# Weight and token preparation moved into the first two attention steps of an attention/convolution branch kernel

## The chip, the cores and the metric

The kernel runs on one core of one Trainium2 chip. The metric is the device time of one execution in microseconds; lower is better. A core has five engines that each work through their own queue in order: TensorE (PE, with its weight loads shown apart as PEld), VectorE (DVE), ScalarE (ACT), GpSimd (POOL) and SyncE (SP), and DMA engines that they issue transfers to. PE and ACT, DVE or POOL meet through semaphores; a waiting instruction holds up everything behind it on its own queue.

## The reference

For two sequences of 4000 tokens with 144 channels, the kernel computes a block and all of its gradients (for x and eight weight tensors). Cut to what matters:

```
xa = layernorm(x)
q, k, v = split(xa @ w_qkv)
p = softmax(q @ k.T * 144**-0.5)
glob = (p @ v) @ w_att_out
u, g = split(gelu(xa @ w_mlp_in))
loc = (u * conv5(layernorm(g), dw_csgu)) @ w_mlp_out
m = concat(glob, loc)
m = m + conv5(m, dw_merge)
out = x + m @ w_merge
```

`conv5` is a depthwise convolution over five tokens. The outputs are `out` and the vector-Jacobian product of this with `grad_out`.

## The kernel before

**Tiling.** Tokens lie as 125 partitions by 32 blocks (`PB` = 125, `NB` = 32). Channels are 128 plus a remainder of 16 (`DR`). The 128 main rows of the transposed normalized tokens are `xaT_m`, those of `grad_out` are `goT`. `R` is one 128-row tile that holds both remainders: the 16 of the tokens, and five shifted copies (80 rows) of those of `grad_out`, so that one matmul takes a remainder and a five-tap sum together.

**Stages.** For each sequence: the prologue (layernorm, transposes, weight products), `phase_att`, then a merge phase (`Merge`). Weights are folded first in `prep_weights`: `M1` is the product of the query and key weights (kept as `Q0`, `RW` and `M1T`), `Wvo` that of value and output weights, `VUT`, `VU` and `VUs` are merge weights times the five taps, `dgm`, `dgf` and `dgs` diagonal matrices for the convolution, `WiT` a transposed weight.

**The prologue of sequence 0**, in this program order: issue the loads of x (SP), build the identity and cleared tiles (POOL), issue the loads of `grad_out` (SP); for each of four groups of eight blocks the statistics (`ln_st`, L318, and `ln_mv`, L324 to L331, which takes a power on POOL, L330) and the normalization (`ln`, L336 on DVE and L338 on POOL); then all of `prep_weights`; then for each group the transposes of tokens (`xat`, L343 to L348) and of `grad_out` (`gs`, L313; `gm`, L306), evicted by ACT and DVE. Two PSUM pools of six buffers serve it (`ps_prep`, `pps`). They are closed before `ps_w` (three buffers) and `ps_yz` are opened.

**`phase_att`** runs 33 steps `t` of eight slots `s`. In step `t`, slots 0 to 3 compute the scores of block `t` (`S_pair`, L683, L684), which DVE turns into a running negative maximum (L688, L690) and ACT into exponentials in `Pbuf` (L691). `rescale` (L696 to L702) aligns the four chunks and issues the DMA transpose `PT` (L703) on SP; the pads of `Pbuf` and `Sbuf` are cleared by POOL with seven DMAs and two memsets (L633, L634). Slots 2 and 3 compute `Y` of block `t-1` from `PT` (L711), slots 4 to 7 its `dP_pair` (L733, L734; DVE L737 to `Sbuf`), followed by the transpose `ST` (L857). Slots 6 and 7 compute `Z` of block `t-2` (L753), and all but slots 2 and 3 accumulate X (L792, DVE L796, L798). `jit_mm` in slot 1 and `jit_tr` in slot 4 prepare block `t+1`: a projection into `qb` (L657) and its four transposes into `qt` (L667). `PT` is a single buffer: the transpose of block `t` waits until Y of block `t-1` has read it.

**Local units.** `local_units` returns a list of small pieces for the convolution branch and its gradient (`z_unit`, L412; `e_tanh`, L420; `dug_unit`, L444; and others). `local()` spreads them evenly over the slots of steps 0 to 30. The first units are PE-light rounds for blocks 30, 31, 0 and 1.

**What sets the order.** Each engine's queue is fixed when the kernel is built, by a scheduler that works through the program by priority. SP and ACT DMAs share eight completion semaphores in turn, so that a ninth DMA waits for the first of them to land. At the end of sequence 1, `F.weights` reads the spilled taps `sWr` again.

Of the kernel before, what the change touches and what calls it, by code (L numbers as in the profile page):

```python
# [7 lines left out]
BF = mybir.dt.bfloat16  # L8
# [100 lines left out]
def prep_weights(k, W):  # L109
    nc, tc = k.nc, k.tc  # L110
    wp, tp_, ps = k.wpool, k.wtmp, k.ps_prep
    ident = W.ident

    def load_k(ap, r0, C, name, eng, pool=None):
        return load_k_(k, pool or wp, ap, r0, C, name, eng)

    dwt = tp_.tile([5, 3 * D], BF, name="dwt")
    nc.scalar.dma_start(dwt[:, 0:2 * D], k.dw_merge)
    nc.scalar.dma_start(dwt[:, 2 * D:3 * D], k.dw_csgu)
    Wqkv = load_k(k.w_qkv, 0, 3 * D, "Wqkv", nc.scalar, tp_)  # L120
    Wo = load_k(k.w_att_out, 0, D, "Wo", nc.scalar, tp_)
    Wm = [load_k(k.w_merge, h * D, D, "Wm%d" % h, nc.scalar, tp_) for h in range(2)]
    Wl = load_k(k.w_mlp_out, 0, D, "Wl", nc.scalar, tp_)
    Wi = load_k(k.w_mlp_in, 0, 2 * D, "Wi", nc.scalar)
    W.Wi = Wi

    def transp(src, c0, name, pool=None):
        t = (pool or wp).tile([128, 2, D], BF, name=name)
        nc.gpsimd.memset(t[:, 1, :], 0.0)
        pt = ps.tile([128, 2, D], BF, tag="tp")  # L130
        for cc, (a, w) in enumerate(((0, 128), (128, DR))):
            nc.tensor.transpose(pt[0:w, cc, 0:128], src[:, 0, c0 + a:c0 + a + w], ident[:])
            nc.tensor.transpose(pt[0:w, cc, 128:D], src[0:DR, 1, c0 + a:c0 + a + w], ident[0:DR, 0:DR])
        nc.scalar.copy(t[:, 0, :], pt[:, 0, :])
        nc.scalar.copy(t[0:DR, 1, :], pt[0:DR, 1, :])
        return t

    W.cols = cols = wp.tile([128, 6, 5], F32, name="cols")
    nc.vector.memset(cols[:], 0.0)
    pc = ps.tile([128, 6, 8], BF, tag="tp")  # L140
    for s, (a, w) in enumerate(((0, 128), (128, DR), (144, 128), (272, DR), (288, 128), (416, DR))):
        nc.tensor.transpose(pc[0:w, s, 0:5], dwt[:, a:a + w], ident[0:5, 0:5])
    for s in range(6):
        w = DR if s % 2 else 128
        nc.vector.tensor_copy(cols[0:w, s, :], pc[0:w, s, 0:5])
    nc.vector.tensor_scalar(cols[:, 0:4, 2:3], cols[:, 0:4, 2:3], 1.0, None, op0=ALU.add)

    WqT = transp(Wqkv, 0, "WqT", tp_)
    WkT = transp(Wqkv, D, "WkT", tp_)
    WvT = transp(Wqkv, 2 * D, "WvT", tp_)  # L150
    WlT = transp(Wl, 0, "WlT", tp_)
    c = float(D) ** -0.5

    def fused(lhs_k, rhs_k, scale, name, pool=None):
        t = (pool or wp).tile([128, 2, D], BF, name=name)
        nc.gpsimd.memset(t[:, 1, :], 0.0)
        for mt, mw in ((0, 128), (1, DR)):
            pt = ps.tile([128, D], F32, tag="tp")
            for kt in range(2):
                nc.tensor.matmul(pt[0:mw, :], lhs_k[:, kt, mt * 128: mt * 128 + mw], rhs_k[:, kt, 0:D], start=(kt == 0), stop=(kt == 1))  # L160
            nc.scalar.activation(t[0:mw, mt, :], pt[0:mw, :], ACT.Copy, scale=scale)
        return t
    M1 = fused(WqT, WkT, c, "M1", tp_)
    W.M1T = fused(WkT, WqT, c, "M1T")
    W.Wvo_d = spill(k, fused(WvT, Wo, 1.0, "Wvo", tp_), "Wvo_d")
    WvoT = fused(Wo, WvT, 1.0, "WvoT", tp_)
    WT = [WvoT, WlT]

    sWm = []
    sWr = []  # L170
    for h in range(2):
        t = tp_.tile([128, 2, 5, D], BF, name="sWm%d" % h)
        for ch in range(2):
            for kk in range(5):
                if h == 0:
                    nc.vector.tensor_scalar(t[:, ch, kk, :], Wm[h][:, ch, :], cols[:, 2 * h + ch, kk:kk + 1], None, op0=ALU.mult)
                else:
                    nc.gpsimd.tensor_scalar(t[:, ch, kk, :], Wm[h][:, ch, :], cols[:, 2 * h + ch, kk:kk + 1], 1.0, op0=ALU.mult, op1=ALU.mult)
        sWm.append(t)
        r = tp_.tile([128, 2, 112], BF, name="sWr%d" % h)  # L180
        nc.gpsimd.memset(r[:, :, 0:32], 0.0)
        for kk in range(5):
            nc.gpsimd.tensor_copy(r[:, :, 32 + (4 - kk) * DR:32 + (5 - kk) * DR], t[:, :, kk, 128:D])
        sWr.append(r)
    W.sWm_d = [spill(k, sWm[h], "sWm_d%d" % h) for h in range(2)]
    W.sWr_d = [spill(k, sWr[h], "sWr_d%d" % h) for h in range(2)]

    W.VUT = wp.tile([128, 5, 2 * D], BF, name="VUT")
    for kk in range(5):
        pt = ps.tile([128, 2, D], F32, tag="vu", name="pt")  # L190
        for h in range(2):
            for ch in range(2):
                nc.tensor.matmul(pt[:, h, :], sWm[h][:, ch, kk, 0:128], WT[h][:, ch, :], start=(ch == 0), stop=(ch == 1))
        (nc.scalar.copy if kk % 2 else nc.vector.tensor_copy)(W.VUT[:, kk, :], pt[:].rearrange("p a b -> p (a b)"))
    W.Q0 = wp.tile([128, D], BF, name="Q0")
    nc.vector.tensor_copy(W.Q0[:], M1[:, 0, :])
    W.RW = wp.tile([128, 3 * D], BF, name="RW")
    nc.gpsimd.memset(W.RW[:], 0.0)
    pt = ps.tile([128, 2, D], F32, tag="vu", name="pt")
    for h in range(2):  # L200
        for ch in range(2):
            nc.tensor.matmul(pt[0:112, h, :], sWr[h][:, ch, :], WT[h][:, ch, :], start=(ch == 0), stop=(ch == 1))
    nc.vector.tensor_copy(W.RW[0:112, D:3 * D], pt[0:112, :, :].rearrange("p a b -> p (a b)"))
    nc.vector.tensor_copy(W.RW[0:DR, 0:D], M1[0:DR, 1, :])

    W.VU = []
    W.VUs = []
    for h in range(2):
        v = tp_.tile([128, 5, D], BF, name="VU%d" % h)
        vf = v[:].rearrange("p a b -> p (a b)")  # L210
        for q in range(2):
            pt = ps.tile([128, 360], F32, tag="vu", name="pt")
            for ch in range(2):
                nc.tensor.matmul(pt[:], WT[h][:, ch, 0:128], sWm[h][:, ch].rearrange("p a b -> p (a b)")[:, q * 360:(q + 1) * 360], start=(ch == 0), stop=(ch == 1))
            (nc.scalar.copy if q else nc.vector.tensor_copy)(vf[:, q * 360:(q + 1) * 360], pt[:])
        W.VU.append(spill(k, v, "VU_d%d" % h))
        sr = tp_.tile([128, 2, 80], BF, name="sr%d" % h)
        for ch in range(2):
            for kk in range(5):
                nc.vector.tensor_scalar(sr[:, ch, kk * DR:(kk + 1) * DR], WT[h][:, ch, 128:D], cols[:, 2 * h + ch, kk:kk + 1], None, op0=ALU.mult)  # L220
        vs = tp_.tile([80, D], BF, name="VUs%d" % h)
        pt = ps.tile([128, D], F32, tag="tp")
        for ch in range(2):
            nc.tensor.matmul(pt[0:80, :], sr[:, ch, :], Wm[h][:, ch, :], start=(ch == 0), stop=(ch == 1))
# [3 lines left out]
    W.WiT = wp.tile([96, 3, D], BF, name="WiT")  # L228
    pt = ps.tile([128, 3, D], BF, tag="tp")
    for ct in range(3):  # L230
        nc.tensor.transpose(pt[0:96, ct, 0:128], Wi[:, 0, ct * 96:(ct + 1) * 96], ident[:])
        nc.tensor.transpose(pt[0:96, ct, 128:D], Wi[0:DR, 1, ct * 96:(ct + 1) * 96], ident[0:DR, 0:DR])
    nc.vector.tensor_copy(W.WiT[:], pt[0:96, :, :])

    mask = tp_.tile([80, DR], BF, name="mask16")
    nc.gpsimd.memset(mask[:], 0.0)
    for r in range(5):
        nc.gpsimd.affine_select(out=mask[:], in_=mask[:], compare_op=ALU.not_equal, fill=1.0, base=-DR * r,
                                pattern=[[-1, DR]], channel_multiplier=1)
    W.mask = wp.tile([80, DR], F32, name="mask32")  # L240
    nc.vector.tensor_copy(W.mask[:], mask[:])
    colS = tp_.tile([80, 2], BF, name="colS")
    with nc.allow_non_contiguous_dma(reason="tiny conv weight column"):
        for kk in range(5):
            nc.sync.dma_start(colS[kk * DR:(kk + 1) * DR, 0:1], k.dw_csgu[kk:kk + 1, 128:D].rearrange("k c -> c k"))
            nc.sync.dma_start(colS[(4 - kk) * DR:(5 - kk) * DR, 1:2], k.dw_csgu[kk:kk + 1, 128:D].rearrange("k c -> c k"))
    colS32 = tp_.tile([80, 2], F32, name="colS32")
    nc.vector.tensor_copy(colS32[:], colS[:])
    W.dgf = wp.tile([128, 5, 128], BF, name="dgf")
    W.dgm = wp.tile([128, 5, 144], BF, name="dgm")  # L250
    for kk in range(5):
# [1207 lines left out]
```

## Time and profile before

| | |
|---|---|
| Median of three runs | 1473.63 us (1470.84 to 1475.2) |
| Profiled execution, its own time | 1475.32 us |
| Span of that execution | 1473.5 us |
| Mean granted TensorE clock | 0.985 |
| Busy, share of the span: PE, PEld, DVE | 93%, 80%, 81% |
| Busy, share of the span: ACT, POOL | 58%, 19% |
| First score matmul (L683) starts | 57.78 us after the span's start |
| First `PT` transposes issued (L703) | 69.03, 80.51, 96.36 and 113.28 us |

Busy times count execution on an engine; a matmul's end is modelled, so a busy PE is not necessarily PE at its peak. "Granted clock" is the TensorE clock as a share of full speed. An arrow `<-` in a row points from the output tile to its inputs, or from a wait to what ended it. In a table of stages the bracket after a busy time is the number of instructions.

### The profile page before, as it was taken

The numbers are of one execution on the slowest core, as the hardware profiler recorded it, in microseconds if no ns is written. First come the engines' busy times: TensorE is split into PE (matmuls) and PEld (weight loads), VectorE is DVE, ScalarE is ACT, GpSimd is POOL, SyncE is SP. The second block draws the span as 40 slices with busy tenths as digits, with TensorE's granted clock in tenths as the row PEclk, the third lists the DMA queues.
The fourth block names the chain that finished last, engine by engine and source line by source line (L and its number), as shares of the span: only waits on it lengthen the run. The fifth ranks groups of instructions, "written<-read, shape, count | busy, mean of one in ns | idle before, by whom it ended". The sixth has DMA issues, their size and how long they took to land. (4 is left out here: it accounts for less than half of the span.)

```text
span 1473.5 us, 38917 instructions
## 1 busy us (share of the span) xinstructions
PE 1374.8 (93%) x16184; PEld 1182.3 (80%) x16184; DVE 1192.4 (81%) x2804; ACT 850.2 (58%) x1538; POOL 282.2 (19%) x494
## 2 busy tenths in 40 slices
PE   2799999999999999997887999999999999999898
PEld 1578888888888888887775888888888888888797
DVE  6688888989888878876738998889898888877754
ACT  1766666666666655632636666666666656564182
POOL 8310111111111110037521112120111010101420
PEclk9989999999999999999999999999999999999999
DMA  3177666666676656577215766677676776666712
GB/s 102 40 135 122 121 122 122 121 122 122 121 120 115 117 104 119 105 144 199 70 48 105 137 123 116 115 118 130 110 128 117 122 121 121 124 120 125 206 34 65
DMA packets 559358, 170.42 MB, mean 116 GB/s; under 512 B 542443, under 2 KB 554093, under 8 KB 559136
## 3 DMA queue, kind: packets, MB, share of 16 engines
q1 hardware_dynamic: 553338, 155.43, 57.0%
q0 software_dynamic: 4768, 12.14, 3.2%
q8 instruction: 126, 2.06, 0.6%
q10 hardware_dynamic: 1076, 0.38, 0.1%
q14 instruction: 50, 0.41, 0.1%
HBM read 21.07 MB, written 14.16 MB: 24 GB/s over the span
## 5 line engine op out<-in xcount | busy, mean ns | idle before, releaser
L737 DVE SCALAR_TENSOR_TENSOR Sbuf<-ps,delta,Pbuf 125x1000 bf16<-125x1000 f32 x256 | 320.1, 1254 | 34.3 <-PE ps L734 32.5
L792 PE MATMUL X<-QBs,Sbuf 125*125 125x144 bf16 x2048 | 302.6, 226 | 5.1 <-DVE acc L798 2.5
L792 PE MATMUL X<-QBs,Pbuf 125*125 125x144 bf16 x2048 | 301.6, 226 | 0.0
L792 PEld LDWEIGHTS <-Pbuf 125*125 125x125 bf16 x2048 | 262.0, 137 | 13.5 <-issue 9.4
L792 PEld LDWEIGHTS <-Sbuf 125*125 125x125 bf16 x2048 | 261.7, 136 | 4.9
L798 DVE TENSOR_TENSOR acc<-X,acc 125x432 f32<-125x432 f32 x372 | 203.6, 550 | 41.9 <-PE X L792 41.2
L683 PE MATMUL ps<-xaT_m,qt 128*125 128x500 bf16 x512 | 192.6, 376 | 14.6 <-ACT Pbuf L691 13.2
L733 PE MATMUL ps<-xaT_m,qt 128*125 128x500 bf16 x512 | 192.2, 375 | 9.4 <-ACT Pbuf L691 6.9
L684 PE MATMUL ps<-R,qt 128*125 128x500 bf16 x512 | 192.1, 375 | 0.0
L734 PE MATMUL ps<-R,qt 128*125 128x500 bf16 x512 | 191.5, 374 | 0.0
L711 PEld LDWEIGHTS <-PT 125*125 125x125 bf16 x2048 | 151.2, 139 | 22.1 <-DMA PT<-Pbuf 4.3
L711 PE MATMUL yz<-xa_aug,PT 125*125 125x145 bf16 x2048 | 154.2, 230 | 2.8 <-DMA PT<-Pbuf 2.8
L753 PEld LDWEIGHTS <-ST 125*125 125x125 bf16 x1984 | 142.9, 137 | 16.3
L753 PE MATMUL yz<-xa_aug,ST 125*125 125x144 bf16 x1984 | 146.8, 228 | 0.0
L684 PEld LDWEIGHTS <-qt 128*125 128x125 bf16 x512 | 69.8, 136 | 37.0 <-issue 16.8
L734 PEld LDWEIGHTS <-qt 128*125 128x125 bf16 x512 | 69.8, 136 | 32.4 <-issue 11.9
L547 POOL TENSOR_TENSOR A_dwc<-l_fl,A_dwc 128x512 f32<-128x512 f32 (+2 forms) x48 | 35.7, 744 | 292.0 <-ACT l_fl L546 292.0
L688 DVE TENSOR_SCALAR_CACHE_REDUCE Pbuf<-ps 125x1000 bf16<-125x1000 f32 x64 | 76.7, 1198 | 18.3 <-PE ps L684 17.8
L683 PEld LDWEIGHTS <-qt 128*125 128x125 bf16 x512 | 69.9, 136 | 21.5 <-ACT qt L667 1.3
L733 PEld LDWEIGHTS <-qt 128*125 128x125 bf16 x512 | 70.0, 137 | 21.1 <-issue 0.6
L757 ACT ACTIVATE zn<-yz,rl 125x144 bf16<-125x144 f32 x64 | 24.1, 377 | 104.5 <-PE yz L753 104.5
L417 POOL TENSOR_SCALAR l_a<-l_sq 125x576 bf16<-125x576 bf16 x32 | 21.5, 670 | 305.1 <-ACT l_sq L415 275.3
(807 smaller groups left out, 3056.0 us busy)
## 6 DMA issues: line engine op xcount, KB each, us to landing
Yn_d<-yn SPq DMA_DIRECT2D x64, 35.2 KB
Zn_d<-zn SPq DMA_DIRECT2D x64, 35.2 KB
ug_d<-ugr SPq DMA_DIRECT2D x32, 70.3 KB
xo<-in_x_dram SPq DMA_DIRECT2D x16, 140.6 KB
out_dram<-dxo SPq DMA_DIRECT2D x16, 140.6 KB
go_h<-in_grad_out_dram POOLq DMA_DIRECT2D x4, 504.0 KB, 7.0
Zn<-Zn_d SPq DMA_DIRECT2D x4, 504.0 KB
PT<-Pbuf SPq DMA_TRANSPOSE x64
```

What stands on the lines that cost most here:

```text
L547: nc.gpsimd.tensor_tensor(acc, fl[0:rows, 0:n], acc, op=ALU.add)
L683: nc.tensor.matmul(ps[:, h, 0:CH], qt[:, 0, :], xaTm[:, cs], start=True, stop=False)
L684: nc.tensor.matmul(ps[:, h, 0:CH], qt[:, 1, :], R[:, cs], start=False, stop=True)
L688: nc.vector.tensor_scalar(pdst, src, -1.0, None, op0=ALU.mult, op1=ALU.min, accum_out=nm[:, 0:1])
L711: nc.tensor.matmul(Y, PT[0:PB, j, 0:PB], xaa[:, j, 0:D + 1], start=(j == 0), stop=(j == NB - 1))
L733: nc.tensor.matmul(ps[:, h, 0:CH], qt[:, 2, :], xaTm[:, cs], start=True, stop=False)
L734: nc.tensor.matmul(ps[:, h, 0:CH], qt[:, 3, :], R[:, cs], start=False, stop=True)
L737: nc.vector.scalar_tensor_tensor(sdst, ps[:, :, 0:CH].rearrange("p h (a b) -> p h a b", b=PB), DL[i][:], psrc, op0=ALU.subtract, op1=ALU.mult)
L753: nc.tensor.matmul(Z, ST[0:PB, j, 0:PB], xaa[:, j, 0:D], start=(j == 0), stop=(j == NB - 1))
L757: nc.scalar.activation(zn[:, 0:D], Z, ACT.Copy, scale=RL.pop(i)[:])
L792: nc.tensor.matmul(X[:, jj, :], l, r, start=(n_ == 0), stop=(n_ == len(ops) - 1))
L798: nc.vector.tensor_tensor(av, X[:, 0:nj, :], av, op=ALU.add)
```

## The change

`prep_weights` becomes a class `Head` with one method for each piece, and `phase_att` of sequence 0 takes a function `head` that emits the prologue within it. Loads, statistics, layernorm, `M1` and the weight pieces that the first scores need come first; the rest (`M1T`, `VUT`, `VU`, the convolution matrices, the `grad_out` transposes) is put into slots of steps 0 and 1 by `steps`. While this is emitted, the order on DVE is the program's (`manual_schedule`), and that on POOL until the end of step 1.

- **Engines.** For sequence 0 half of the layernorm, and all ten taps of the first merge weight, go to ACT (before: POOL and DVE). Taps of the second half stay on POOL. The `sr` products, masks and `dgm`, `dgs` go from DVE to POOL, and ten tiny `colS` loads from SP to POOL. Evictions of `VUT`, `VU`, `RW`, `cols`, `WiT` all go to ACT.
- **DMA.** The loads of `w_merge` go from ACT to SP, between those of x and of `grad_out`. Weights land in one tile `raw` that DVE clears early.
- **PSUM.** The prologue uses the three buffers of `ps_w`.
- **Split first projection.** `jit_q` and `jit_b` compute the score half and the gradient half of block 0 separately, since the second half needs `VUT` and `goT`.
- **Remainder rows.** Token remainders move from rows 0 to 15 of `R` to rows 96 to 111, those of `grad_out` from 32 to 0; `sWr` shrinks from 112 to 80 columns. The zero-padded `qb` becomes a tile without padding and a small tile `qrr`, which costs one more ACT copy for each block in both sequences.
- **Local units** of sequence 0 start in step 2 and are spread over steps 2 to 30.

```diff
+        ld(self.Wqkv, k.w_qkv, 0)
+        ld(self.Wo, k.w_att_out, 0)
+        nc.scalar.dma_start(self.dwt[:, 0:2 * D], k.dw_merge)
+        nc.scalar.dma_start(self.dwt[:, 2 * D:3 * D], k.dw_csgu)
+        ld(self.Wl, k.w_mlp_out, 0)
+        for h in range(2):
+            ld(self.Wm[h], k.w_merge, h * D, nc.sync)
+        nc.scalar.dma_start(W.Wi[0:128, 0, :], k.w_mlp_in[0:128, :])
+        nc.scalar.dma_start(W.Wi[96:96 + DR, 1, :], k.w_mlp_in[128:D, :])
+        nc.scalar.dma_start(self.Wi2[:], k.w_mlp_in[128:D, :])
...
+            if h == 0:
+                nc.scalar.activation(t[:, ch, kk, :], self.Wm[h][:, ch, :], ACT.Copy, scale=col)
+            else:
+                nc.gpsimd.tensor_scalar(t[:, ch, kk, :], self.Wm[h][:, ch, :], col, 1.0, op0=ALU.mult, op1=ALU.mult)
...
-                if j % 2:
+                if S.act_ln and j % 2 == 0:
+                    nc.scalar.activation(S.xa_aug[:, j, 0:D], x_tp[:, j, :], ACT.Identity, scale=S.rstd_x[:, j:j + 1], bias=nmr[:, j:j + 1])
+                elif S.act_ln or j % 2:
...
-                nc.tensor.transpose(pr[0:DR, bi, 0:PB], S.xa_aug[:, 8 * g + bi, 128:D], W.ident[0:PB, 0:PB])
-            nc.vector.tensor_copy(v8(S.R, 8 * g, 8)[0:DR], pr[0:DR, :, 0:PB])
+                nc.tensor.transpose(pr[0:112, bi, 0:PB], S.xa_aug[:, 8 * g + bi, 32:D], W.ident[0:PB, 0:PB])
+            nc.vector.tensor_copy(v8(S.R, 8 * g, 8)[96:112], pr[96:112, :, 0:PB])
...
-            nc.scalar.copy(qb[:, :, 0:D], pj[:].rearrange("p (a b) -> p a b", b=D))
+            nc.scalar.copy(qb[:], pj[:].rearrange("p (a b) -> p a b", b=D))
+            nc.scalar.copy(qrr[i % 3][:, :, 96:112], pj[:].rearrange("p (a b) -> p a b", b=D)[:, :, 128:D])
...
+                if head is not None and t == 2 and s == 0:
+                    units += local_units(k, W, b, S, A, es_loc, DHT, ps_w)
+                    n_units, u0 = len(units), 2
+                if head is not None and t < 2:
+                    for f in steps[8 * t + s]:
+                        f()
...
-                local(-(-n_units * (8 * t + s + 1) // (8 * (NB - 1))))
+                if t >= u0:
+                    local(-(-n_units * (8 * (t - u0) + s + 1) // (8 * (NB - 1 - u0))))
...
+        with tc.manual_schedule(engines={nc.vector.engine}):
+            for n in ("st0", "mv0", "st1", "mv1"):
+                P[n]()
+            hd.m1()
+            hd.cols()
+            P["ln0"]()
+            hd.taps(1, 0, 4)
+            for n in ("st2", "mv2", "xat0"):
+                P[n]()
+            f["jit_q"]()
+            hd.vo()
+            P["ln1"]()
+            hd.taps(1, 4, 8)
+            for n in ("st3", "mv3", "xat1"):
+                P[n]()
+            hd.taps(0)
+            P["ln2"]()
+            hd.taps(1, 8, 10)
+            hd.tapr(1)
+            hd.tapr(0)
+            P["xat2"]()
+            P["gr"]()
+            P["ln3"]()
+            clear()
+            f["pads"]()
+        steps = [[] for _ in range(16)]
+        steps[0] = []
+        steps[1] = [hd.m1t]
+        steps[2] = [hd.vut]
+        steps[3] = [P["xat3"], P["gs0"], P["gma"], P["gm0"]]
+        steps[4] = [f["jit_b"], P["gs1"]]
+        steps[5] = [P["gm1"], f["jit_1"]]
+        steps[6] = [P["gs2"], P["gm2"], lambda: hd.vu(0)]
+        steps[9] = [P["gs3"], P["gm3"], P["gmb"], lambda: hd.vu(1)]
+        steps[12] = [hd.conv, clear_a]
+        steps[15] = [es_p0.close, k.head_order.close]
```

## The prediction

> **What bounds the kernel now.** I read the table of stages first. Columns: window, its length, then busy us (instructions) of PE, PEld, DVE, ACT and POOL, granted clock, DMA share, GB/s.
>
> ```profile
> 0.00:57.80 57.80, 26.67 (x253) 19.93 (x253) 36.41 (x145) 18.66 (x42) 39.88 (x97) 0.97 0.28 78
> 57.80:69.00 11.20, 7.61 (x49) 5.11 (x50) 9.30 (x24) 9.94 (x17) 1.29 (x2) 1.00 0.00 0
> 69.00:80.50 11.50, 8.67 (x44) 6.05 (x44) 5.49 (x12) 8.02 (x12) 2.17 (x5) 0.59 0.61 106
> 80.50:96.40 15.90, 14.72 (x117) 10.81 (x116) 15.82 (x34) 9.87 (x18) 1.16 (x3) 0.98 0.77 145
> 205.80:600.00 394.20, 387.12 (x4521) 332.04 (x4520) 339.64 (x720) 245.10 (x441) 46.96 (x73) 1.00 0.66 119
> ```
>
> The steady stretch (last row) is PE's: 387.12 of 394.20 us, ACT 62% busy. The first row is nobody's: PE idles 57.80 − 26.67 = 31.1 us, DVE 21.4, ACT 39.1. In the next two rows PE idles 3.6 and 2.8. So up to about 37 us could go before the first step is full; afterwards PE has 1.2 us of slack in a step, then less.
>
> The timeline (start, duration, engine, line, operation) gives the marks:
>
> ```profile
> 57.78 0.42 PE L683 MATMUL ps<-xaT_m,qt 128*125 128x500 bf16 x1 [0.35 <-ACT qt L667]
> 69.03 4.96 SPq L703 DMA_TRANSPOSE PT<-Pbuf  x1
> ...
> 80.51 4.97 SPq L703 DMA_TRANSPOSE PT<-Pbuf  x1
> ```
>
> The first scores start at 57.78, PT(0) goes out 11.3 us later, PT(1) at 80.51. From PT(1) on the same work stands in both kernels' queues, apart from the moved units and the new copy, so I compare the time of PT(1).
>
> **Part 1: when ACT is free.** In the changed queues ACT issues eight weight loads first; the one of the remainder of `Wi` shares a completion semaphore with the seventh load of x and waits for it.
>
> ```profile
> 6.28 0.35 SPq L41 DMA_DIRECT2D x_tp<-in_x_dram  x1
> ```
>
> The first load of x was issued at 0.75 and used at 4.09, so 3.3 us; the seventh lands at about 6.28 + 3.3 = 9.6. Behind this wait stands everything that ACT does, evictions of the first weight transposes included. Before, ACT began at 14.22, so even this is no loss, but it starts the sum.
>
> **Part 2: ACT's queue to PT(0).** Half of layernorm leaves POOL (16 × 0.47) for ACT, the ten taps of the first merge half leave DVE (2.7) for ACT, and evictions shared with DVE come to ACT. Rows by form (count | busy, mean ns | idle before):
>
> ```profile
> L454 ACT ACTIVATE gd<-l_hg,rsr 125x144 bf16<-125x144 bf16 x6 | 2.8, 496 | 3.4 <-DVE rsr L452 3.4
> L344 ACT COPY xaT_m<-pt 128x1000 bf16<-128x1000 bf16 x4 | 4.0, 994 | 0.2 <-PE pt L343 0.2
> L307 ACT COPY goT<-pt 128x1000 bf16<-128x1000 bf16 x4 | 4.0, 992 | 2.9 <-PE pt L306 2.8
> L691 ACT ACTIVATE Pbuf<-ps,nm__944 125x1000 bf16<-125x1000 f32 x4 | 4.4, 1090 | 1.3 <-DVE Pbuf L690 1.3
> ```
>
> No ACT layernorm exists in this trace; the nearest row, with scale and bias read from tiles at the same 125x144, is `gd`: 16 × 0.496 = 7.9. Taps between the plain copy (0.28) and 0.496: 2.8 to 5.0, I take 3.8. In queue order: transposed weights 0.8, layernorm 7.9, `Q0` and `RW` 0.6, `cols` 0.8, taps 3.8, `xaT` 4 × 0.99 = 4.0, first `qb`/`qrr`/`qt` 0.9, `WvT`, `WlT` 1.1, `WvoT` 0.6, `M1T` 0.6, `RW` 0.4, `VUT` 5 × 0.4 = 2.0, `goT` 0.4 + 1.0, `jit_b` 0.9, exponentials 4 × 1.1 = 4.4, `f` 0.3, `goT` 1.0, rescale 1.1. Sum 32.5; 9.6 + 32.5 gives PT(0) at 42 (before: 69.03).
>
> Beside it: DVE's written order sums to 31 us from 4.1, so 35, with statistics, half of layernorm and remainder copies; hidden by 7. POOL's (powers 4 × 1.65, taps 10 × 0.40, copies, seven pads whose DMAs it issues at 0.52 and that land in 4.4) ends at 33 to 35; also hidden. If either cover were gone, each us over 42 counts whole. SP's queue gains the two `w_merge` loads between x and `grad_out`, 0.9 of issue; `grad_out` is first read after 25, so 10 us cover them.
>
> **Part 3: step 1.** PT(1) needs Y(0) to have read the single PT buffer.
>
> ```profile
> 76.29 4.03 PE L711 MATMUL yz<-xa_aug,PT 125*125 125x145 bf16 x31 [0.78 <-DMA PT<-Pbuf]
> ```
>
> From PT's issue to Y's start: 76.29 − 69.03 = 7.26. Y at full clock is 32 × 0.064 = 2.04 (here 4.03 at a granted clock of 0.5). So 9.3 at least; ACT's other work before it (7.0: `goT`, `VU`, exponentials) is hidden under that. ACT work after it in its queue (`goT`, `VUs`, two convolution evictions, exponentials and rescale of block 1) is about 8.3. PT(1) at 42 + 9.3 + 8.3 = 59.7, against 80.51: **−20.8**. POOL's chain (20 `sr` products at 0.20, mask, ten `colS` loads at 0.42 issue, `dgm`, `dgs`, clears, `gd`) ends at about 55.5; cover 4 us. If it is late, DVE L420 waits for POOL L417 behind it, and the local rounds of step 2 with it.
>
> **Part 4: units two steps later.** Before, steps 0 and 1 carried rounds for two groups: PE 2.5 us, DVE 2 × 3.9 = 7.8. They now fall into steps 2 to 30, where the stage rows show DVE at 15.82 of 15.90 at first and 86% later. Loss 2.5 (PE alone) to 7.8 (DVE alone); half of the steps' DVE work finds room: **+4**.
>
> **Part 5: the extra copy.** One `qrr` copy a block, 62 in all, at 0.263 (16x144 row of L135) to 0.40 (`qb`, L657): 16 to 25 us more of ACT. What PE loses to ACT today, from the table of waits over 131 to 640 us (us, times, longest):
>
> ```profile
> PE ps L733 <- ACT Pbuf L691: 2.2, 5, 0.8
> PE X L792 <- DVE acc L798: 1.3, 2, 0.6
> PE ps L683 <- ACT Pbuf L691: 1.0, 2, 0.8
> PE pw L579 <- ACT qt L667: 0.6, 1, 0.6
> ```
>
> Some 5 us of 509 for all ACT waits: the copy lies beside PE. I take **+1**; bounds 0 and 25. Padding `R` differently changes no matmul's moving size; `qb`'s memsets on POOL vanish before the loop, hidden. The smaller `sWr` reload at the end is priced 0 within ±1.
>
> **Sum**, against the profiled execution of 1475.3: 1475.3 − 20.8 + 4 + 1 = 1459.5. The median lies 1.7 lower: **1458**. Cross-check by PE: of 37 us idle, 42 + 18 less PE's unchanged 43 busy leaves about 17, so 20 gained, less parts 4 and 5: 15.
>
> **The rivals.**
>
> *Overlapping ACT (1452).* Successive copies start 0.17 apart though each lasts 0.28:
>
> ```profile
> 15.52 0.28 ACT L134 COPY WqT<-pt 128x144 bf16<-128x144 bf16 x1
> 15.69 0.26 ACT L135 COPY WqT<-pt 16x144 bf16<-16x144 bf16 x1
> ```
>
> If all of the some 60 small operations of parts 2 and 3 did that, 60 × 0.1 = 6 less: 1452. Against it: most wait for PE or DVE between, as the three later pairs of L134 do, 0.8 each.
> The Trainium skill states such an overlap of back-to-back ACTIVATEs, about 93 ns each (ScalarE: Activation LUTs, What ACT_TABLE_LOAD costs); 60 of them would be an estimated 5.6 us, and the rows above agree at 0.11.
>
> *Half clock (1468).* The stage of 69 to 80.5 granted 0.59, after PE waited; a transfer-bound step 1 with fewer fillers may keep it low. Scores of blocks 0 and 1 take 2 × 3.4 = 6.8 instead of 3.4 (8 × 0.21 a block), Y 2.0 more, dP and the `grad_out` transposes about 5 more: 10.4, to 1468. Against it: transposes now sit between the waits.
> The Trainium skill describes this re-throttling when a thin kernel's waits recur (TensorE: Matmul & The Clock Gate, HAM oscillation); this trace agrees with the 0.59.
>
> *No gain (1473).* Three PSUM buffers in place of twelve make PE, ACT and DVE take turns: some 50 evictions, each exposing an extra 0.3 (a copy's 0.28), 15 in all. Then the change moves but does not overlap the prologue. Against it: PE had six and idled anyway.
>
> *Slower (1482).* In each step `qrr` stands in ACT's queue ahead of the exponentials; ACT waits precede both rows of `ps` above. If ACT becomes the last releaser of every step, 62 × 0.40 = 24.8 goes on the path, against −20.8 + 4: 1475.3 + 8.0 − 1.7 = 1482. It decides once ACT's slack in a step (38% of 18.7 us = 7) sits elsewhere than where the copy falls. For it: PE has 2% slack only, so any new wait counts. Against it: only 5 us of waits in 509.
>
> **How the numbers follow.** Forecast 0.58, overlapping ACT 0.09, half clock 0.11, no gain 0.10, slower 0.12. A measurement of this kernel tells about 0.3% (4.4 us) from no change. Faster: 0.55 of the forecast's share, 0.09, and 0.08 of half clock = 0.72. Same: the rest of these and 0.07 of no gain = 0.13. Slower: 0.12 and 0.03 = 0.15. The range goes from 1448 (overlap, 1452, with part 4 at its lower bound, 1.5 less, part 5 at 0, 1 less, and the reload's 1) to 1476 (no gain and its margin); the slower rival stays outside. The forecast's own range is 1452 to 1466.
>
> **What the new profile would show.** Right: PT(0) near 42, PT(1) near 60, steps of 18.7 us from 200 on, PE's waits for ACT still under 1% there. First scores near 30, ACT over 85% busy until 42. Wrong in part 1: ACT's first copy well off 9.6. Part 2: DVE or POOL as last releaser of the first scores. Part 3: Y(0) long after PT landed, or L420 waiting for POOL. Part 4: PT(4) gains much less than PT(1). Part 5: a new wait of PE for `Pbuf` or `qt` in every step. A clock below 0.8 over the first 60 us shows the second rival.

## The result, and the profile after

The changed kernel takes 1465.49 us (median of six runs, 1460.56 to 1468.35) against 1474.22 before (six runs, 1470.84 to 1475.2): a ratio of 0.9941, 95% interval 0.9922 to 0.9960. So it is faster by 0.6%, where 1.1% was forecast; the median lies just inside the upper end of the forecast's own range (1452 to 1466). The profiled execution took 1460.56 us with a span of 1458.8 at a mean granted clock of 0.987; it is the fastest of the six, and that of before (1475.32) lies above all six of its kernel, so the two traces differ by 14.8 us where the medians differ by 8.7.

The marks that the prediction used, from the timeline of the changed kernel (start, duration, engine, line, operation):

```profile
41.10 5.22 SPq L760 DMA_TRANSPOSE PT<-Pbuf  x1
...
62.39 4.85 SPq L760 DMA_TRANSPOSE PT<-Pbuf  x1
...
76.13 4.79 SPq L760 DMA_TRANSPOSE PT<-Pbuf  x1
```

PT(0), PT(1) and PT(2) go out at 41.10, 62.39 and 76.13, before at 69.03, 80.51 and 96.36: 27.9, 18.1 and 20.2 us sooner. The table of stages of the same execution, columns as in the prediction:

```profile
0.00:10.10 10.10, 1.42 (x8) 0.85 (x9) 7.44 (x33) 1.58 (x3) 6.35 (x21) 1.00 0.56 148
10.10:41.10 31.00, 22.84 (x183) 16.61 (x182) 19.53 (x63) 27.13 (x68) 23.85 (x64) 0.89 0.29 80
41.10:62.40 21.30, 17.47 (x144) 12.70 (x145) 10.82 (x19) 13.59 (x26) 9.93 (x25) 0.92 0.36 75
62.40:76.13 13.73, 12.14 (x110) 9.22 (x109) 11.92 (x25) 10.64 (x19) 1.77 (x3) 1.00 0.84 157
```

From 10.1 to 41.1 ACT is busy 27.13 of 31.00 us, more than any other engine: ACT is now the busiest engine of the prologue. PE idles 8.7 + 8.2 + 3.8 = 20.7 us in the first three rows, up to PT(1), against 37.5 up to the same event before.

Following each PT through both traces shows where the gain went. Differences of after to before in us, each read off the timelines:

| block of PT | after | before | difference |
|---|---|---|---|
| 2 | 76.13 | 96.36 | −20.2 |
| 12 | 261.09 | 281.48 | −20.4 |
| 18 | 378.90 | 391.88 | −13.0 |
| 31, last of sequence 0 | 628.87 | 642.59 | −13.7 |
| 0 of sequence 1 | 755.60 | 780.90 | −25.3 |
| 3 of sequence 1 | 810.49 | 824.51 | −14.0 |
| 31 of sequence 1 | 1338.81 | 1353.97 | −15.2 |
| end of the span | 1458.8 | 1473.5 | −14.7 |

The head gains 20; from block 13 on (−16.3 there) some 7 go again; at the start of sequence 1 eleven more are won and lost at once. The experiments take these one by one.

### The profile page after: what moved, and what is told of

It is laid out like the page before. It is cut to its first block, busy times and chain, and to the rows that moved or that the text cites. A ratio compares the mean times of both kernels' runs of the same rounds, so it can differ in the third digit from the quotient of the medians.

```text
span 1458.8 us, 38954 instructions
## 1 busy us (share of the span) xinstructions
PE 1373.0 (94%) x16185; PEld 1180.9 (81%) x16185; DVE 1177.4 (81%) x2747; ACT 866.6 (59%) x1641; POOL 284.6 (20%) x507
## 5 line engine op out<-in xcount | busy, mean ns | idle before, releaser
L849 PEld LDWEIGHTS <-Pbuf 125*125 125x125 bf16 x2048 | 262.0, 137 | 15.2 <-issue 10.8
L768 PE MATMUL yz<-xa_aug,PT 125*125 125x145 bf16 x2048 | 151.9, 228 | 10.5 <-DMA PT<-Pbuf 10.4
L741 PEld LDWEIGHTS <-qt 128*125 128x125 bf16 x512 | 70.2, 137 | 30.0 <-issue 10.4
L740 PEld LDWEIGHTS <-qt 128*125 128x125 bf16 x512 | 70.3, 137 | 20.4 <-ACT qt L724 0.6
```

The lines of the kernel that those rows point to most:

```text
L740: nc.tensor.matmul(ps[:, h, 0:CH], qt[:, 0, :], xaTm[:, cs], start=True, stop=False)
L741: nc.tensor.matmul(ps[:, h, 0:CH], qt[:, 1, :], R[:, cs], start=False, stop=True)
L768: nc.tensor.matmul(Y, PT[0:PB, j, 0:PB], xaa[:, j, 0:D + 1], start=(j == 0), stop=(j == NB - 1))
L849: nc.tensor.matmul(X[:, jj, :], l, r, start=(n_ == 0), stop=(n_ == len(ops) - 1))
```

## The experiments

### The changed kernel again, and the units alone

e1 is the changed kernel unedited.

> The changed kernel once more. The one profiled execution was 14.8 us under the profiled one of before, the medians only 8.7. If that is spread between executions of the same program, the median stays near 1465 (1460 to 1468), PT(1) again goes out near 62 us and PT(12) near 261, and what is lost of the 20 us falls at other steps than 12 to 18. If it is structural, the profile shows the same 4 to 5 us lost in steps 12 to 18 of sequence 0.

It took 1464.87 us (1463.96 to 1466.93) against 1474.17, ratio 0.9928 (0.9916 to 0.9941). In its trace PT(2), PT(12), PT(18) and PT(31) are at 76.5, 261.4, 379.2 and 629.2, each 0.3 to 0.4 later than in the first trace. So the loss between 12 and 18 is structural: it comes again in a second execution. What differs between the two executions lies elsewhere: from PT(31) to the first PT of sequence 1 it is 130.1 us instead of 126.7, and after the last PT 122.3 instead of 120.0.

e2 is the kernel before, with its units held back:

```diff
-                local(-(-n_units * (8 * t + s + 1) // (8 * (NB - 1))))
+                u0 = 2 if b == 0 else 0
+                if t >= u0:
+                    local(-(-n_units * (8 * (t - u0) + s + 1) // (8 * (NB - 1 - u0))))
```

> The kernel before with only the local units of sequence 0 held back to step 2. My term for this: 4 us, so 1478. PE alone would ask 2.5 (1476.5), DVE alone 7.8 (1482). If deferral is free: 1474.

It took 1482.56 us, ratio 1.0060 (1.0042 to 1.0078): 8.4 us slower by the medians. Its trace is the longest of its six executions (1489.84), so only sequence 0 is read from it. Two rows of the table of stages, from PT(2) to PT(31), first the kernel before, then e2:

```profile
96.36:642.59 546.23, 537.76 (x6264) 460.71 (x6263) 473.77 (x1012) 341.69 (x613) 65.71 (x102) 1.00 0.66 119
```

```profile
96.43:649.65 553.22, 541.66 (x6289) 463.45 (x6288) 478.59 (x1030) 347.69 (x629) 69.73 (x111) 1.00 0.66 118
```

The stretch is 7.0 us longer. PE's busy time grew by 3.9, so 3.1 more are PE's idle time: the moved rounds bring PE work, and in steps that are already full they also bring waits. DVE grew by 4.8. The 7.0 is near the DVE bound of the prediction (7.8), not half of it; but DVE was given only 4.8 more, so that nearness does not show that DVE sets the price. In the tables of waits of the two stretches PE's waits grow in small pieces: those for DVE are 2.7 instead of 1.3, and one of 1.0 for a PT is new. The loss falls between the same blocks: e2 is 0.4 behind at PT(12), 4.5 at PT(13), 7.7 at PT(18), and swings between 4.5 and 8.7 from there on. Against e2, PT(2) of the changed kernel is 20.3 sooner, and every PT from block 4 to block 31 between 20.6 and 20.8: without the units' price, the head's gain is kept to the end of sequence 0.

### The extra copy

e3 adds the copy to the kernel before (into a tile that nothing reads). e4 takes it out of the changed one from block 2 on, and so leaves out the 16 remainder channels of these projections:

```diff
             nc.scalar.copy(qb[:, :, 0:D], pj[:].rearrange("p (a b) -> p a b", b=D))
+            nc.scalar.copy(qxr[i % 3][:, :, 96:112], pj[:].rearrange("p (a b) -> p a b", b=D)[:, :, 128:D])
```

```diff
-            nc.scalar.copy(qrr[i % 3][:, :, 96:112], pj[:].rearrange("p (a b) -> p a b", b=D)[:, :, 128:D])
+            if i < 2:
+                nc.scalar.copy(qrr[i % 3][:, :, 96:112], pj[:].rearrange("p (a b) -> p a b", b=D)[:, :, 128:D])
```

> The kernel before with one more ACT copy of the projection's remainder per block, into a tile that nothing reads. My term: 1 us, so 1475. If the copy stands on the path it costs 62 times 0.21 (its length in the changed kernel) = 13 us, so 1487, and would explain the missing 6 us of the median at half that.

> The changed kernel without the remainder copy from block 2 on in both sequences, so the 16 remainder channels of the projections are left out of scores and dP there. My term: 1 us, so 1464 where the changed kernel has 1465. If the copy costs what the median lacks: 1459.

e3: 1473.03 us, ratio 0.9998 (0.9987 to 1.0010). e4: 1465.22, ratio 0.9934 (0.9922 to 0.9946), where e1, against the same runs of the kernel before, has 0.9928. The copy costs nothing that can be told; its PTs in e3 lie within 0.2 us of those of before through all of sequence 0 from block 2 on. The rival that was to end slower is out.

### Spreading, order, and the two small waits of the head

e7 emits every piece ahead of step 0:

```diff
             steps = head(...)
+            for st_ in steps:
+                for f in st_:
+                    f()
+            steps = [[] for _ in range(16)]
```

> The changed kernel with every piece emitted ahead of step 0, nothing put into slots of steps 0 and 1; engines, queues of loads, remainder rows and held-back units stay. If the gain of 20.7 us in the first steps comes from overlap of scores and preparation, most of it goes: PT(2) 10 to 15 us later, 1475 to 1480. If it comes from engines and loads being better used, PT(2) moves by under 5 and the time is below 1470.

1479.41 us, ratio 1.0042 (1.0028 to 1.0056). The timeline of its SP queue:

```profile
60.51 15.90 SPq L760 DMA_TRANSPOSE PT<-Pbuf  x2
...
87.98 4.78 SPq L760 DMA_TRANSPOSE PT<-Pbuf  x1
```

The first row holds PT(0) and PT(1); PT(2) goes out at 87.98, 11.9 us later than in the changed kernel and 8.4 sooner than before. So of the 20.2 us at PT(2) the spreading is worth 11.9, and engines, loads and order 8.4. At PT(31) of sequence 0 e7 is still 1.3 us ahead of the kernel before; that it ends slower comes from behind that, from the start of sequence 1 (2.9) and from what follows the last PT (2.4).

e8 takes out both hand-written orders (`manual_schedule` for GpSimd and VectorE).

> The changed kernel without the order written out for VectorE and GpSimd; the scheduler orders them. My sum had both engines hidden under ACT by 7 us: then PT(0) stays within 2 us of 41 and the time within 2 of 1465. If the order matters, PT(0) is later by what the last of them waits, 5 us or more.

1466.67 us, ratio 0.9954 (0.9935 to 0.9973). PT(0) goes out at 44.87, 3.8 later, PT(1) at 61.20, 1.2 sooner, PT(31) at 632.2, 3.3 later than in the changed kernel. The order moves the first steps by a few us; the time cannot tell it from none.

e11 moves ACT's two loads of the remainder of `w_mlp_in` to SP:

```diff
-        nc.scalar.dma_start(W.Wi[96:96 + DR, 1, :], k.w_mlp_in[128:D, :])
-        nc.scalar.dma_start(self.Wi2[:], k.w_mlp_in[128:D, :])
+        nc.sync.dma_start(W.Wi[96:96 + DR, 1, :], k.w_mlp_in[128:D, :])
+        nc.sync.dma_start(self.Wi2[:], k.w_mlp_in[128:D, :])
```

> The changed kernel with the two small loads of w_mlp_in's remainder on SP behind w_merge instead of on ACT, so that ACT's first evictions do not wait for a load of x (1.8 us in its trace). My sum makes ACT's queue set PT(0): then PT(0) goes out 1.5 to 2 us sooner and the time is 1463. If something else sets PT(0): unchanged, 41 and 1465.

1465.24 us, ratio 0.9948 (0.9929 to 0.9967). ACT's timeline around the wait, first of the changed kernel, then of e11:

```profile
8.01 0.28 ACT L160 COPY two<-hps 128x144 bf16<-128x144 bf16 x1
9.72 0.32 ACTq L150 DMA_DIRECT2D Wi<-in_w_mlp_in_dram  x1
10.08 0.27 ACT L161 COPY two<-hps 16x144 bf16<-16x144 bf16 x1 [1.79 <-DMA x_tp<-in_x_dram]
10.25 0.26 ACT L160 COPY two<-hps 128x144 bf16<-128x144 bf16 x1
```

```profile
8.03 0.26 ACT L161 COPY two<-hps 16x144 bf16<-16x144 bf16 x1
...
10.37 0.90 ACT L382 ACTIVATE xa_aug<-x_tp,lnnm,rstd_x 125x144 bf16<-125x144 bf16 x2 [1.74 <-DVE lnnm L377]
```

The wait for the load of x (1.79) is gone, and one of 1.74 for DVE's statistics stands in its place. PT(0) goes out at 40.33, only 0.8 sooner. So ACT's queue is not alone in setting PT(0): here the statistics end at nearly the same time as the load that ACT waited for.

e6 issues the ten `colS` loads on SP behind those of `grad_out`:

```diff
-                nc.gpsimd.dma_start(colS[kk * DR:(kk + 1) * DR, 0:1], ...)
-                nc.gpsimd.dma_start(colS[(4 - kk) * DR:(5 - kk) * DR, 1:2], ...)
...
+                nc.sync.dma_start(colS[kk * DR:(kk + 1) * DR, 0:1], ...)
+                nc.sync.dma_start(colS[(4 - kk) * DR:(5 - kk) * DR, 1:2], ...)
```

> The changed kernel with its ten colS loads issued on SP behind the loads of grad_out instead of on POOL in step 1. In the changed kernel they are issued in the same microseconds as PT(0), and Y(0) starts 9.6 us after PT(0) goes out, where the kernel before needed 7.3. If the colS loads delay the transpose: Y(0) 7.3 us after PT(0), PT(1) near 60, 1462.5. If not, 9.6 stays and the time too.

1465.93 us, ratio 0.9950 (0.9930 to 0.9969). In the changed kernel the loads are issued from 40.28 to 45.14, around PT(0) at 41.10, and PE waits for PT:

```profile
50.63 0.18 POOL L292 CAST colS<-colS 80x2 f32<-80x2 bf16 x1 [5.49 <-DMA colS<-in_dw_csgu_dram]
50.73 1.23 PE L768 MATMUL yz<-xa_aug,PT 125*125 125x145 bf16 x16 [1.78 <-DMA PT<-Pbuf]
```

In e6 PT(0) goes out at 41.14, and:

```profile
49.23 1.23 PE L772 MATMUL yz<-xa_aug,PT 125*125 125x145 bf16 x16 [0.24 <-DMA PT<-Pbuf]
```

From PT(0) to Y(0) it is 8.1 us instead of 9.6: the loads cost 1.5 of the 2.4 that are more than the 7.26 of before. PT(1) and PT(2) are 1.4 sooner; but PT(3) is at 96.06 instead of 94.33, and the rest stays behind. What is won in one step is given back in the next.

e5 starts the units in slot 4 of step 1, with the convolution pieces two slots earlier:

```diff
-                if head is not None and t == 2 and s == 0:
+                if head is not None and t == 1 and s == 4:
...
-        steps[12] = [hd.conv, clear_a]
-        steps[15] = [es_p0.close, k.head_order.close]
+        steps[10] = [hd.conv, clear_a]
+        steps[11] = [es_p0.close, k.head_order.close]
```

> The changed kernel with the convolution pieces two slots earlier and the local units starting in slot 4 of step 1 instead of step 2 (232 slots become 236). Holding units back cost the kernel before 7.1 us in the trace and 8.4 in the median. If that is because PE and DVE work leaves steps that had room, part of it comes back in the half step: PT(2) later by less than 2 us, PT(31) earlier, 1460 to 1464. If the room of step 1 is already used by the head, nothing is won: 1465 to 1468.

1466.06 us, ratio 0.9947 (0.9927 to 0.9967). PT(2) goes out at 81.55, 5.4 later than in the changed kernel, PT(31) at 633.2, 4.3 later. The edit moves the convolution pieces too, so the two are not told apart; together they find no room in step 1.

### The start of sequence 1

The traces of kernels with the head have a short way from the last PT of sequence 0 to the first of sequence 1 (126.7 to 130.1 us in the changed kernel, e1, e4, e8 and e11; 136.9 to 138.3 before, in e3 and e9), and a long one over the next three blocks (54.9 to 55.8 against 41.7 to 43.6). The sum is 183.7 against 180.4 on the mean: 3.3 us lost. Single traces spread as widely as that (181.6 to 185.5 against 178.6 to 181.9), and the first pair shows no loss (181.6 against 181.9), so the 3.3 is a mean of a few traces and no more. The three steps in the table of stages, before:

```profile
780.90:791.60 10.70, 6.79 (x45) 5.26 (x45) 5.48 (x12) 7.97 (x12) 2.18 (x5) 0.84 0.57 111
791.60:807.80 16.20, 14.18 (x116) 10.55 (x115) 15.79 (x34) 9.84 (x18) 1.27 (x3) 1.00 0.78 144
807.80:824.50 16.70, 16.36 (x189) 13.97 (x188) 16.51 (x36) 11.89 (x22) 3.37 (x6) 1.00 0.73 138
```

and after:

```profile
755.60:764.70 9.10, 7.23 (x64) 5.20 (x63) 4.46 (x9) 6.01 (x9) 0.00 (x0) 1.00 0.62 115
764.70:789.10 24.40, 18.20 (x146) 13.59 (x147) 20.91 (x49) 16.54 (x33) 5.24 (x10) 0.93 0.50 95
789.10:810.50 21.40, 17.03 (x165) 13.85 (x163) 16.16 (x36) 12.34 (x23) 3.61 (x7) 0.92 0.63 115
```

The second step took 16.2 and takes 24.4: DVE does 20.9 us in it where it did 15.8, and PE idles 6.2 there and 4.4 in the third, where it idled 2.0 and 0.3. Scores start sooner, and the rounds of units fall on top of them. Of the 11.3 us that the three steps are longer, 5.1 are PE's own work (42.5 instead of 37.3) and 6.2 its idle time. The table of waits names what most of the new idle time waits for (total us, times, longest); first before, then after:

```profile
PE yz L711 <- DMA PT<-Pbuf: 1.1, 1, 1.1
```

```profile
PE yz L768 <- DMA PT<-Pbuf: 5.2, 2, 4.1
```

e1, e8 and e11 have 5.3, 5.3 and 6.2 there, e9 and e12 1.1. The longest wait ends at 799.01, 9.9 us after that PT was issued, and right ahead of this PT on SP's queue stands a transfer that belongs to the units:

```profile
788.30 0.64 SPq L512 DMA_DIRECT2D gd<-gd  x1
789.11 6.07 SPq L760 DMA_TRANSPOSE PT<-Pbuf  x1
```

In the kernel before the same transfer goes out 5.8 us behind a PT (797.36 after 791.57). No run moves this transfer alone, so its part in the wait is not shown.

e9 asks whether the moved rows do this: the kernel before with their layout and `qb` split, prologue and units as they were.

```diff
-                nc.tensor.transpose(pr[0:DR, bi, 0:PB], S.xa_aug[:, 8 * g + bi, 128:D], W.ident[0:PB, 0:PB])
-            nc.vector.tensor_copy(v8(S.R, 8 * g, 8)[0:DR], pr[0:DR, :, 0:PB])
+                nc.tensor.transpose(pr[0:112, bi, 0:PB], S.xa_aug[:, 8 * g + bi, 32:D], W.ident[0:PB, 0:PB])
+            nc.vector.tensor_copy(v8(S.R, 8 * g, 8)[96:112], pr[96:112, :, 0:PB])
...
-            nc.tensor.matmul(pt[0:112, h, :], sWr[h][:, ch, :], WT[h][:, ch, :], start=(ch == 0), stop=(ch == 1))
+            nc.tensor.matmul(pt[0:80, h, :], sWr[h][:, ch, :], WT[h][:, ch, :], start=(ch == 0), stop=(ch == 1))
```

> The kernel before with only the remainder rows moved (tokens to rows 96 to 111 of R, grad_out from row 0, small sWr, the unpadded qb with its extra copy); prologue, engines and units as before. In all traces of changed kernels sequence 1 starts its first PT about 9 us sooner after the last one of sequence 0 and then needs 11.5 us more for the next three steps (55 instead of 43.5). In the old layout the rows of grad_out overwrite row 0 to 15, so tokens must come after them. If the layout does this: the same two figures here, and 1474 to 1478. If the new order in the prologue does it: 138 and 43.5 as before, and 1474.

1473.79 us, ratio 1.0001 (0.9991 to 1.0010), with 136.9 and 41.7 us. The layout costs and brings nothing by itself, and does not make the long start. e8 has it too (127.5 and 55.3), so the written order does not; which part of the new prologue does stays open.

e10 lets the units of sequence 1 begin one step later in the changed kernel, e12 does the same in the kernel before:

```diff
-        units, u0 = [], 0
+        units, u0 = [], 0 if head is not None else 1
```

```diff
-                local(-(-n_units * (8 * t + s + 1) // (8 * (NB - 1))))
+                u0 = 1 if b == 1 else 0
+                if t >= u0:
+                    local(-(-n_units * (8 * (t - u0) + s + 1) // (8 * (NB - 1 - u0))))
```

> The changed kernel with the local units of sequence 1 starting in step 1 instead of step 0. If the first steps of sequence 1 are long because units wait for grad_out and pile up, they get shorter by 3 to 8 us, and 4 come back later as in sequence 0: 1460 to 1466. If they are long for another reason: 1467 to 1470.

> The kernel before with the local units of sequence 1 starting in step 1. If the 8 us that this won on the changed kernel are time that its long first steps of sequence 1 had lost, there is nothing of that here (its three steps take 43.5 us) and the later steps pay: 1474 to 1479. If the later start is simply better for any kernel: 1466 to 1468.

e10 takes 1457.53 us (1453.72 to 1460.99), ratio 0.9885 (0.9869 to 0.9901): below both kernels, and its interval lies clear of that of the changed kernel. e12 takes 1473.14, ratio 0.9992 (0.9981 to 1.0004). So the later start wins nothing in the kernel before; it pays only with the new prologue, and there it wins more than the 3.3 us above. The same three steps in e10:

```profile
759.70:770.60 10.90, 8.73 (x48) 5.85 (x47) 4.52 (x9) 5.46 (x6) 0.00 (x0) 0.69 0.52 96
770.60:791.00 20.40, 15.69 (x120) 11.71 (x121) 17.40 (x38) 13.02 (x24) 3.63 (x7) 0.92 0.60 114
791.00:808.20 17.20, 16.72 (x174) 13.83 (x173) 16.63 (x36) 12.19 (x25) 3.25 (x6) 1.00 0.82 136
```

They take 48.5 us instead of 54.9, and 5.1 of the difference are PE's idle time: the `gd` transfer now goes out 5.6 us behind the PT (796.67 after 791.03), and the table of waits lists none for PT. The later steps of sequence 1 take 1.5 more (529.8 instead of 528.3). That is 5 of the 8 us between the medians; e10's trace is the longest of its four executions (span 1459.2), and no trace here shows the remaining 3.

## Why the prediction was right, and where its size was off

The sign, the mechanism and the range were right; the gain was 8.7 us of the 15.6 forecast. Two terms were too small, and one place, the start of sequence 1, was not in the sum.

**Part 1** held: ACT's wait for a load of x ended at 10.08 (9.6 forecast), though one eviction ran ahead of it, at 8.01. **Part 2** gave the right time partly by luck: PT(0) at 41.10 (42), but ACT was busy 27.13 us of the 32.5 summed (the terms as listed add to 32.6), and waited 3.9 for others. The first scores were further off, at 21.3 where the prediction looked for 30. ACT's rows by form:

```profile
L382 ACT ACTIVATE xa_aug<-x_tp,lnnm,rstd_x 125x144 bf16<-125x144 bf16 x16 | 7.3, 498 | 0.2
...
L392 ACT COPY xaT_m<-pt 128x1000 bf16<-128x1000 bf16 x4 | 4.0, 991 | 1.0 <-PE pt L391 1.0
L217 ACT ACTIVATE sWm<-raw,cols 128x144 bf16<-128x144 bf16 x10 | 3.3, 402 | 0.0
```

The nearest row was a good price for one instruction (0.496 for 0.498), but the sum took no overlap: 16 of 0.498 are 8.0, and the row holds 7.3. The copies at 10.08 and 10.25 above last 0.27 and start 0.17 apart. The Trainium skill (ScalarE: Activation LUTs, What ACT_TABLE_LOAD costs) gives about 93 ns of overlap for ACTIVATEs that follow one another; these rows, of plain copies, agree with 0.10. So the first rival was right about the overlap (32.5 − 27.1, some 5 us) and wrong about the result, since waits took most of it back; e11 shows for one of them that the next stood right behind it.

**Part 3** was mis-sized by 3.7: PT(0) to PT(1) took 21.3 us, 17.6 were summed. Of this, 2.4 lie between PT(0) and Y(0), where the ten small loads were priced on POOL's time (1.5 by e6) and not on the transfer that they run beside; the rest of the 3.7 is not traced to a cause. POOL itself was covered, as said: its last head instruction ended at 56.7, before PT(1). At PT(1), where the forecast stood, the gain was 18.1 us instead of 20.8. At PT(2) it was 20.2, since the next step took 13.7 us where it took 15.9; in e2, with the units held back alone, it took 15.6, so the moved units do not explain that. That the head's gain came out near 20.8 in the end is luck.

**Part 4** is the term that failed: 4 us were taken between 2.5 and 7.8, and e2 measured 7.0 in its trace and 8.4 in its median. The reason given, that half of the DVE work finds room in later steps, was wrong; PE was busy 98% there, and the moved rounds brought 3.9 us of PE work (2.5 were counted) and 3.1 of waits.

**Part 5** held: the copy is 0.20 us long (27 of them 5.4 us on ACT) and costs nothing (e3, e4). PE's waits for ACT stayed where they were, over 131 to 640 us:

```profile
PE ps L790 <- ACT Pbuf L748: 2.0, 6, 0.5
...
PE ps L740 <- ACT Pbuf L748: 0.8, 1, 0.8
```

**What the sum did not have** is sequence 1. It was taken as unchanged, apart from the copies; its start loses 3.3 us by the means above, with waits for PT, and e10 wins that back and more.

Together, by traces: −13.5 at PT(31) of sequence 0 (the head's 20.7 less the units' 7.1), +3.3 at the start of sequence 1, −1.1 in its other steps (528.4 instead of 529.5), +0.9 behind the last PT (120.5 instead of 119.6, means of the traces named above): −10.4. The medians gave −8.7 and, in e1, −9.3; a us or two of spread is left, and the terms behind sequence 0 are means of three to five traces that spread as widely as they differ.

**The rivals.** Half clock: the stages show 0.89 and 0.92, and the first 60 us 0.91 where below 0.8 was to show this rival; so the clock dipped in places, and the gain at PT(2) came all the same. No gain: the preparation does overlap with the scores in spite of three PSUM buffers, by the 11.9 us of e7 at PT(2). Slower by the copy: out (e3, e4).

## What to carry to other kernels

When work is moved out of the first steps of a loop whose bounding engine is full, price it at no less than the moved work's whole time on that engine, and add the waits that it brings: here 3.9 us of PE work cost 7.0. The deferral can be run alone in the old kernel to measure this. A gain at the start of the program does not pass through a kernel unchanged: follow one repeated event (here the issue of PT) block by block through both traces, and look at every place where the order of the queues comes out anew, as at the second sequence.

## What was not expected of the hardware

Within the attention steps two executions of the same kernel repeat to within 0.2 us relative to each other, over 550 us (e1 is 0.2 to 0.4 behind the first trace from PT(2) to PT(31)). Their spans differ by 6.4 us, and nearly all of it arises in two other stretches: between the sequences (126.7 and 130.1 us) and behind the last block (120.0 and 122.3). One pair of profiled executions therefore gave 14.8 us where the medians gave 8.7, while the differences inside the steps could be read to a few tenths. Whether this holds beyond these two traces is not shown.
